# A shared score tile with nine products instead of twelve, row sums turned in spare columns, and products with V dealt 9 9 9 9 6 6 6 9 9

## The chip, the core and the metric

The kernel runs on one core of a Trainium2 chip. TensorE (PE in the profile, PEld for its weight loads) multiplies, VectorE (DVE) and ScalarE (ACT) read its results from PSUM, GpSimd (POOL) works on SBUF alone, and SyncE (SP) issues the DMAs. The metric is the device time of one execution in microseconds (us), the median of several runs; smaller is better.

## The reference

Three blocks follow each other. The change lies in the first.

```python
# q, k, v: (2, 8, 1152, 64) float32
q_pool = q.reshape(B, H, S // 2, 2, D).mean(axis=3)          # 576 query rows per head
scores = scale * np.matmul(q_pool, k.transpose(0, 1, 3, 2))  # 576 x 1152 per head
attn = np.exp(scores - np.max(scores, axis=-1, keepdims=True))
attn = attn / (np.sum(attn, axis=-1, keepdims=True) + 1e-09)
attn_out = np.matmul(attn, v)                                # 16 heads
# then x (1152 x 512) -> ELU block (512 -> 2048 -> 512)
# then RMS norm -> gated SiLU block (512 -> 1536 -> 512)
```

## The kernel before

Nearly every product is made of three: each fp32 operand is split into a high part in the fast format fp32r and a low part (the rest, again in fp32r), and high x high, high x low and low x high are added up in PSUM. `hi_...` makes a high part, `lo_...` subtracts it to make the low one (lines 60 to 70; these lines stand for all such operations in the profile: L61 and L64 on POOL, L67 and L70 on DVE).

The attention half works on pairs of heads, p = 0 to 7, with j = 0 and 1 for the two heads of a pair. Keys lie in a tile `kd` of 128 partitions: the high part of the 64 rows in partitions 0 to 63, the low part in 64 to 127. Queries (the pooled sum of two rows, in 576 columns) lie in `qt`: 128 partitions that hold the same 64 rows twice, once as high part (u = 0) and once as low part (u = 1), so a score tile of 128 queries takes two products over 1152 keys, each cut into three matmuls of 384 columns: six matmuls. A head has 576 queries, four tiles of 128 and a rest of 64. The rests of both heads of a pair share one tile, number 2 (`M`): its queries are set off by zero columns, and it takes both heads' two products, twelve matmuls.

One step of the loop (line 580) handles one score tile, nine steps to a pair:

- PE: the scores of this step's tile into the PSUM tile `s` (`emit_S`, L350; three banks, one buffer);
- PE: nine transposes of the tile two steps back (`do_T`, `emit_T`, L368; three PSUM buffers `t`);
- PE: eight products with V (`do_AV`, L394), taken from a queue of groups. A group has 18: nine blocks of keys, each with the high and the low part of the weights. A pair has four groups, two of 256 and two of 320 columns; a group enters the queue when the last of its tiles has been transposed. Where the next group is not there yet, fewer are issued; where a transpose would overwrite what a waiting group still reads, the rest of that group is issued first;
- DVE: one reduction that takes the scores out of PSUM and finds the row's extreme (L354), three subtractions for the transposed tile (L70), an addition where a group of 256 columns ends (L414);
- ACT: three casts of the transposed tile (L376), copies where a group ends (L407 to L413), the exponential with the row sum (L359);
- POOL: a preparation of q, k or v for the pairs to come, by the table `plan` (L487); SP fetches the raw array of the preparation that follows (`fetch`; two buffers for raw k and v together, two for raw q).

When all nine tiles of a pair are transposed, `emit_r` takes the reciprocals of the row sums. They lie along partitions and are needed along columns: POOL spreads them (`rs`), four transposes turn eight of the nine columns two steps after the pair's last product with V, a further transpose the ninth column a step later (`emit_scale`, L433 and L438), ACT copies them out of PSUM into `xs`. In the steps in which that is due, the transposes of the score tile come after the products with V and not before them. `emit_x` then scales the pair's output on POOL and splits it. In pair 0 the tiles come in the order 0 1 3 4 2 5 6 7 8, in the others as 0 to 8. In some steps (`early_ops`) weights of the next half are converted ahead.

Of the kernel before, what the change touches and what calls it, by code (L numbers as in the profile page):

```python
# [39 lines left out]
def tile_kernel(ctx: ExitStack, tc: tile.TileContext, qd, kd, vd, w1d, w2d, wgd, wvd, wod, rgd, outd):  # L40
# [229 lines left out]
    qt = [ap.tile([128, 2, 704], F32R, name=f"qt{i}", tag=f"qt{i}") for i in range(3)]  # L270
# [5 lines left out]
    for z in qt:  # L276
        V.memset(f(z[:, :, 0:64]), 0.0)
        V.memset(f(z[:, :, 640:704]), 0.0)
    V.memset(ones, 1.0)

# [19 lines left out]
    def prep_q(p, j, t, eng, cols=((0, QS),)):  # L300
# [4 lines left out]
        d, qp = QD[p, j], t[:, 0, :]  # L305
# [18 lines left out]
    def prep_v(p, j, t, eng):  # L324
        hi, lo = eng
        d = VD[p, j] = ap.tile([128, 9, 128], F32R, tag="vd", name="vd", bufs=3)
# [4 lines left out]

    st = {}
# [3 lines left out]
    def emit_S(p, i):  # L336
# [3 lines left out]
        if i == M:  # L340
            parts = [(QD[p, j][:, u, c:c + 128], KD[p, j]) for j, c in ((1, 0), (0, 576)) for u in (0, 1)]
        else:
            j, c, _, _, _ = TILES[i]
            parts = [(QD[p, j][:, u, c:c + 128], KD[p, j]) for u in (0, 1)]
# [17 lines left out]
    def emit_T(p, i):  # L362
        src = P.pop((p, i)).rearrange("p a b -> p (a b)")
        for g in range(3):
            ps = tbank()[:, 0:384].rearrange("p (k c) -> p k c", k=3)
# [10 lines left out]
            T.copy(oh, re(ps))  # L376
            lo_dve(ol, re(ps), oh)
# [40 lines left out]
    def emit_r(p):  # L418
        s = st[p]
        V.tensor_scalar(out=s[:, 2], in0=s[:, 1], scalar1=1e-9, scalar2=None, op0=ALU.add)  # L420
        V.reciprocal(s[:, 3], s[:, 2])
        rs[p] = ap.tile([128, 640], F32, tag="xs", name="rs", bufs=1)[:, 0:512].rearrange("p (a b) -> p a b", a=8)
        hi_pool(rs[p], s[:, 3, 0:8].to_broadcast([128, 8, 64]))
# [58 lines left out]
    def fetch(u):  # L482
        if u not in raws:
# [3 lines left out]
    plan = {1: lambda p: ("v", p, 0), 2: lambda p: ("q", p + 1, 1), 3: lambda p: ("k", p + 1, 1, 0),  # L487
            4: lambda p: ("k", p + 1, 1, 1), 5: lambda p: ("v", p + 1, 1), 6: lambda p: ("q", p + 1, 0),
            7: lambda p: ("k", p + 1, 0, 0), 8: lambda p: ("k", p + 1, 0, 1)}
    steps = [(p, i) for p in range(8) for i in ([0, 1, 3, 4, 2, 5, 6, 7, 8] if p == 0 else range(NPT))]  # L490
    ns = len(steps)
    jobs = {n: [] for n in range(-1, ns)}
    for n in range(ns):
# [4 lines left out]
        if k in plan and not (p == 0 and k == 1):  # L498
# [81 lines left out]
    for step in range(ns):  # L580
# [14 lines left out]
        if step >= LT and due:  # L595
            do_T(step)
# [507 lines left out]
```

## Time and profile before

| | us |
|---|---|
| median of 3 runs (lowest, highest) | 667.93 (667.74, 668.16) |
| span of the profiled execution | 666.8 |
| from the first score matmul of pair 2 to that of pair 7 | 148.73 |
| PE, DVE, ACT, POOL busy in the whole span | 659.0, 511.5, 465.2, 443.6 |

The span is that of one profiled execution, from its first instruction to its last; the timed runs are 1.1 us longer, with what lies around the span. A matmul's record shows when it started and a modelled end, and records overlap: what a matmul costs in a sequence is the distance between starts. In the timeline, neighbouring records of one kind are merged, with their number behind the x; "idle before" in brackets names what ended a wait.

### The profile page before, as it was taken

Reading aid. Unit: us, or ns where it says so; the run is one execution under the profiler, and the core shown is the slowest. Engines: PE = TensorE matmul, PEld = TensorE weight load, DVE = VectorE, ACT = ScalarE, POOL = GpSimd, SP = SyncE. Lnnn points to the kernel's source line nnn. Section 1 sums busy time; section 2 is a strip of 40 time slices with the busy share of each in tenths; the row PEclk is TensorE's granted clock in tenths of the full one; section 3 lists DMA queues with packets and bytes.
Section 4 is the critical chain, followed back from the end, with each engine's and each line's share of the span. In section 5 each row is a group of like instructions: output and inputs, shape, how many; then the busy total and the mean of one; then the engine's idle time right before and its main releaser. Section 6 shows DMA issues by size and latency. Waiting matters only on the chain.

```text
span 666.8 us, 11391 instructions
## 1 busy us (share of the span) xinstructions
PE 659.0 (99%) x4149; PEld 652.1 (98%) x4149; DVE 511.5 (77%) x884; ACT 465.2 (70%) x910; POOL 443.6 (67%) x407
## 2 busy tenths in 40 slices
PE   7999999999999999999999999999999999999997
PEld 6999999999999999999999999999999999999997
DVE  7989898998999878987786787688697786676200
ACT  6988888898988977848758668866766654564300
POOL 4999888989989323758776695665998874404200
PEclk9999999999999999999999999999999999999999
DMA  6432333233223101142141232110323322204100
GB/s 177 171 107 90 108 131 133 90 108 121 90 89 94 46 1 64 43 148 95 64 158 65 94 129 94 65 64 32 126 96 125 129 94 68 91 1 162 68 36 36
DMA packets 21624, 61.75 MB, mean 93 GB/s; under 512 B 2752, under 2 KB 5056, under 8 KB 21568
## 3 DMA queue, kind: packets, MB, share of 16 engines
q1 hardware_dynamic: 21568, 61.03, 27.9%
q8 instruction: 32, 0.52, 0.3%
q14 instruction: 24, 0.20, 0.1%
HBM read 58.66 MB, written 2.36 MB: 92 GB/s over the span
## 4 chain that ended last, share of the span: by engine, by line
PE 96%; POOL 1%; DVE 1%; DMA 1%; issue 0%; SPq 0%; ACT 0%; POOLq 0%; ACTq 0%
PE b L747 17%; PE b L217 14%; PE b L219 14%; PE b L218 14%; PE s L350 12%; PE o L394 11%; PE t L368 10%; DMA rawq<-in_q_dram 1%; PE t L433 1%; DVE p L354 0%; POOL kd L64 0%; POOL qt L64 0%; PE fb L217 0%; PE fb L219 0%; PE fb L218 0%
## 5 line engine op out<-in xcount | busy, mean ns | idle before, releaser
L64 POOL TENSOR_TENSOR wl<-wt,wh 128x512 fp32r<-128x512 f32 x68 | 91.1, 1340 | 83.9 <-ACT wh L184 79.0
L70 DVE TENSOR_TENSOR ptl<-t,pth 128x384 fp32r<-128x384 f32 x216 | 106.7, 549 | 4.9 <-ACT pth L376 4.5
L354 DVE TENSOR_SCALAR_CACHE_REDUCE p<-s 128x1152 f32<-128x1152 f32 x72 | 97.4, 1354 | 15.1 <-PE s L350 13.7
L376 ACT CAST pth<-t 128x384 fp32r<-128x384 f32 x216 | 89.2, 488 | 22.3 <-PE t L368 21.6
L350 PE MATMUL s<-kd,qt 128*128 128x384 f32 x480 | 98.7, 342 | 2.9 <-DVE p L354 1.4
L359 ACT ACTIVATE p<-p,st 128x1152 f32<-128x1152 f32 x72 | 91.5, 1271 | 0.5 <-DVE p L354 0.2
L217 PE MATMUL b<-xh,wh 128*128 128x384 f32 x260 | 87.7, 337 | 0.0
L350 PEld LDWEIGHTS s<-kd,qt 128*128 128x128 f32 x480 | 81.0, 188 | 6.6 <-DVE p L354 2.8
L219 PE MATMUL b<-xh,wl 128*128 128x384 f32 x260 | 87.5, 336 | 0.0
L218 PE MATMUL b<-xl,wh 128*128 128x384 f32 x260 | 87.4, 336 | 0.0
L394 PE MATMUL o<-pth,vd 128*128 128x256 f32 (+1 forms) x288 | 84.4, 315 | 0.0
L368 PE MATMUL t<-ident,p 128*128 128x128 f32 x648 | 82.5, 272 | 0.0
L394 PE MATMUL o<-ptl,vd 128*128 128x256 f32 (+1 forms) x288 | 78.6, 295 | 0.0
L368 PEld LDWEIGHTS t<-ident,p 128*128 128x128 f32 x648 | 75.0, 141 | 1.8
L120 ACT ACTIVATE we<-wr 128x512 uint32<-128x512 uint32 x68 | 45.4, 667 | 38.8 <-DMA wr<-in_w_dram 19.1
L131 DVE TENSOR_SCALAR wm<-wm 128x512 f32<-128x512 f32 x63 | 43.8, 695 | 20.3 <-ACT wm L122 20.3
L394 PEld LDWEIGHTS o<-pth,vd 128*128 128x128 f32 x288 | 54.3, 189 | 0.3
L122 ACT ACTIVATE wm<-wr 128x512 f32<-128x512 f32 x63 | 39.6, 628 | 21.4 <-DVE wt L136 21.3
L394 PEld LDWEIGHTS o<-ptl,vd 128*128 128x128 f32 x288 | 54.5, 189 | 0.0
L218 PEld LDWEIGHTS b<-xl,wh 128*128 128x128 f32 x260 | 48.8, 188 | 0.0
L217 PEld LDWEIGHTS b<-xh,wh 128*128 128x128 f32 x260 | 48.8, 188 | 0.0
L219 PEld LDWEIGHTS b<-xh,wl 128*128 128x128 f32 x260 | 48.8, 188 | 0.0
(198 smaller groups left out, 1750.6 us busy)
## 6 DMA issues: line engine op xcount, KB each, us to landing
wr<-in_w_dram SPq DMA_DIRECT2D x32, 512.0 KB, 3.2
rawq<-in_q_dram SPq DMA_DIRECT2D x15, 576.0 KB, 4.0
rawk<-in_k_dram SPq DMA_DIRECT2D x28, 288.0 KB, 2.9
wr<-in_wg_dram SPq DMA_DIRECT2D x12, 512.0 KB, 3.2
wr<-in_wv_dram SPq DMA_DIRECT2D x12, 512.0 KB, 3.2
wr<-in_wo_dram SPq DMA_DIRECT2D x12, 512.0 KB, 3.2
rawv<-in_v_dram SPq DMA_DIRECT2D x16, 288.0 KB, 2.9
out_dram<-o SPq DMA_DIRECT2D x12, 192.0 KB, 1.8
```

The source lines that it names most:

```text
L64: G.tensor_tensor(out=o, in0=i, in1=f(h), op=ALU.subtract)
L70: V.tensor_tensor(out=o, in0=i, in1=f(h), op=ALU.subtract)
L217: PE.matmul(out, lhsT=wh[:, k, :], rhs=ah, start=first and k == 0, stop=False)
L218: PE.matmul(out, lhsT=wh[:, k, :], rhs=al, start=False, stop=False)
L219: PE.matmul(out, lhsT=wl[:, k, :], rhs=ah, start=False, stop=last and k == 3)
L350: PE.matmul(s[:, m, 0:384], lhsT=a, rhs=b[:, 384 * m:384 * m + 384], start=n == 0, stop=n == len(parts) - 1)
L354: V.tensor_scalar(out=pt, in0=s[:, :, 0:384], scalar1=-0.0625, scalar2=None, op0=ALU.mult, op1=ALU.min, accum_out=st[p][:, 0, TILES[i][4], :])
L359: T.activation(out=pt, in_=pt, func=AF.Exp, scale=-1.0, bias=st[p][:, 0, TILES[i][4], :], accum_out=st[p][:, 1, TILES[i][4], :])
L368: PE.transpose(ps[:, k, :], src[:, 128 * b:128 * b + 128], ident)
L376: T.copy(oh, re(ps))
L394: PE.matmul(self.o[:, 0:self.N], lhsT=v[:, b, :], rhs=(pth, ptl)[u][:, g["buf"], b, g["c0"]:320], start=self.n == 0, stop=self.n == 17)
L747: PE.matmul(out, lhsT=a[x][:, k, :], rhs=b[y][:, k, :], start=first and (k, x, y) == (0, 0, 0), stop=last and (k, x, y) == (1, 1, 0), skip ...
```

## The change

The shared tile takes nine matmuls. Both rests' high parts are multiplied with the keys as before (two products, six matmuls). The two products with low parts become one: the low parts of both heads' rests stand in one 128 x 128 tile `bd`, head 1's in partitions 0 to 63 and columns 64 to 127, head 0's in partitions 64 to 127 and columns 0 to 63, zeros elsewhere, and a tile `zd` holds the high parts of both heads' keys, one above the other. `zd` is filled by two DMAs per pair from SBUF to SBUF (`stack_k`). The low part of the queries, now a tile of its own, no longer needs the rest's columns, which go into `bd` by a subtraction of their own.

The row sums are turned by one transpose of a 128 x 128 tile `rc` into unused columns (384 to 511) of the third PSUM buffer of a score tile's transposes; ACT copies nine rows back; five DMAs write them in the right order to DRAM, and two DMAs read them back, spread over 64 partitions each (`store_r`, `load_r`). The last pair keeps the old way. The scaling follows three steps after the last product with V, as before.

All pairs take the tiles in the order 0 1 3 4 2 5 6 7 8. The products with V are dealt out 9 9 9 9 6 6 6 9 9 over the nine steps. The score tile's transposes always come before the products with V. V of head 1 is prepared in the pair's second step, V of head 0 in its sixth (before: head 0 in the second, head 1 of the next pair in the sixth), with two buffers instead of three.

```diff
-    qt = [ap.tile([128, 2, 704], F32R, name=f"qt{i}", tag=f"qt{i}") for i in range(3)]
+    qt = [(ap.tile([128, 704], F32R, name=f"qh{i}", tag=f"qh{i}"), ap.tile([128, QS], F32R, name=f"ql{i}", tag=f"ql{i}"))
+          for i in range(3)]
+    bds = [ap.tile([128, 128], F32R, name=f"bd{i}", tag=f"bd{i}") for i in range(2)]
...
+    for z in bds:
+        G.memset(f(z), 0.0)
     V.memset(ones, 1.0)
+    rc = ap.tile([128, 128], F32, name="rc")
+    G.memset(rc, 1.0)
...
-            h, l = (d[:, u, 64 + a:64 + b] for u in range(2))
-            hi(h, qp[:, a:b])
-            lo(l, qp[:, a:b], h)
+            hi(h[:, 64 + a:64 + b], qp[:, a:b])
+            if a <= m < b:
+                lo(bds[p % 2][r, o:o + 64], qp[r, m:m + 64], h[r, 64 + m:128 + m])
+            for a, b in ((a, min(b, 512)),) if m else ((max(a, 64), b),):
+                if a < b:
+                    lo(l[:, a:b], qp[:, a:b], h[:, 64 + a:64 + b])
+
+    ZD = {}
+
+    def stack_k(p, j):
+
+        if p not in ZD:
+            ZD[p] = ap.tile([128, S], F32R, tag="zd", name="zd", bufs=1)
+        SP.dma_start(out=f(ZD[p][64 * (1 - j):64 * (2 - j)]), in_=f(KD[p, j][0:64]))
...
-            parts = [(QD[p, j][:, u, c:c + 128], KD[p, j]) for j, c in ((1, 0), (0, 576)) for u in (0, 1)]
+            parts = [(QD[p, j][0][:, c:c + 128], KD[p, j]) for j, c in ((1, 0), (0, 576))] + [(bds[p % 2], ZD[p])]
...
+            if turn and g == 2:
+                PE.transpose(bank[:, 384:512], rc, ident)
...
             T.copy(oh, re(ps))
+            if turn and g == 2:
+                T.copy(rc[0:NPT], bank[0:NPT, 384:512])
             lo_dve(ol, re(ps), oh)
...
+        V.reciprocal(rc[:, 0:NPT], s[:, 2].rearrange("p a b -> p (a b)"))
+        later.extend([(step + 1, rows), (step + 2, lambda: store_r(p)), (step + 3, lambda: load_r(p))])
...
+    def store_r(p):
+
+        d = RD[p] = dp.tile([2, QS], F32, tag="rd", name="rd", bufs=2)
+        for j in range(2):
+            for k in range(2):
+                n = j + 4 * k
+                SP.dma_start(out=d[j:j + 1, 320 * k:320 * k + 256].rearrange("p (k c) -> (p k) c", k=2), in_=rc[n:n + 3:2, :])
+        SP.dma_start(out=d[:, 256:320], in_=rc[8:9, :].rearrange("p (j c) -> p j c", j=2))
+
+    def load_r(p):
+        d = RD.pop(p)
+        xs = XS[p] = ap.tile([128, 640], F32, tag="xs", name="xs", bufs=1)
+        for j in range(2):
+            SP.dma_start(out=xs[64 * j:64 * j + 64, 0:QS], in_=d[j:j + 1, :].to_broadcast([64, QS]))
...
-    steps = [(p, i) for p in range(8) for i in ([0, 1, 3, 4, 2, 5, 6, 7, 8] if p == 0 else range(NPT))]
+    steps = [(p, i) for p in range(8) for i in (0, 1, 3, 4, 2, 5, 6, 7, 8)]
...
-        if step >= LT and not due:
+        due, done = [w for w in later if w[0] <= step and w[1] is not rows], []
+        if step >= LT:
             do_T(step)
...
-        do_AV(8, lambda p: later.extend([(step + 2, lambda: emit_scale(p, (0,))),
-                                        (step + 3, lambda: emit_x(p, emit_scale(p, (1,))))]), done)
-        if step >= LT and due:
-            do_T(step)
+        do_AV((9, 9, 9, 9, 6, 6, 6, 9, 9)[step % NPT], lambda p: later.append((step + 3, lambda: emit_x(p, XS[p]))), done)
...
+        for u in jobs.get(step - 2, []):
+            if u[0] == "k" and u[3] == 1:
+                stack_k(u[1], u[2])
```

In the program, PE's queue of pair 1 around the shared tile before (s is the PSUM tile of scores, qt_91 and qt_93 the queries of both heads, t the transposes, o the products with V):

```order
L350 MATMUL s<-kd,qt_93 128x384 x6
L350 MATMUL s<-kd,qt_91 128x384 x6
L394 MATMUL o<-pth,vd 128x320
L394 MATMUL o<-ptl,vd 128x320
L368 MATMUL t<-ident,p 128x128 x9
L394 MATMUL o<-pth,vd 128x256
L394 MATMUL o<-ptl,vd 128x256
```

The same place after:

```order
L369 MATMUL s<-kd,qh_95 128x384 x3
L369 MATMUL s<-kd,qh_91 128x384 x3
L369 MATMUL s<-zd,bd_98 128x384 x3
L390 MATMUL t<-ident,p 128x128 x9
L420 MATMUL o<-pth,vd 128x256
L420 MATMUL o<-ptl,vd 128x256
L420 MATMUL o<-pth,vd 128x256
L420 MATMUL o<-ptl,vd 128x256
L420 MATMUL o<-pth,vd 128x256
L420 MATMUL o<-ptl,vd 128x256
```

Twelve score matmuls became nine, the last three on `zd`, and a whole step's six products follow the transposes.

PE's queue where pair 0's row sums are turned, before (in pair 1's seventh and eighth steps):

```order
L350 MATMUL s<-kd,qt_91 128x384 x6
L433 MATMUL t<-ident,rs 128x128 x4
L394 MATMUL o<-pth,vd 128x256
L394 MATMUL o<-ptl,vd 128x256
L394 MATMUL o<-pth,vd 128x256
L394 MATMUL o<-ptl,vd 128x256
L368 MATMUL t<-ident,p 128x128 x9
L350 MATMUL s<-kd,qt_91 128x384 x6
L438 MATMUL t<-ident,st 128x128
L394 MATMUL o<-pth,vd 128x320
```

And after (in pair 1's third step):

```order
L369 MATMUL s<-kd,qh_95 128x384 x3
L369 MATMUL s<-kd,ql_96 128x384 x3
L390 MATMUL t<-ident,p 128x128 x9
L392 MATMUL t<-ident,rc 128x128
L420 MATMUL o<-pth,vd 128x256
```

The five transposes became one behind a score tile's nine, and these stand ahead of the products in every step.

SP's queue at the start, before (the rows from the load of the norm's weights on):

```order
L532 DMA rg<-in_rg_dram 128x4
L286 DMA rawq<-in_q_dram 128x1152
L294 DMA rawk<-in_k_dram 128x576 x2
L93 DMA wr<-in_w_dram 128x1024 x2
L297 DMA rawv<-in_v_dram 128x576
```

And after, up to the first turn of row sums:

```order
L579 DMA rg<-in_rg_dram 128x4
L328 DMA zd<-kd 64x1152 x2
L292 DMA rawq<-in_q_dram 128x1152
L300 DMA rawk<-in_k_dram 128x576 x2
L93 DMA wr<-in_w_dram 128x1024 x2
L292 DMA rawq<-in_q_dram 128x1152
L300 DMA rawk<-in_k_dram 128x576
L328 DMA zd<-kd 64x1152
L300 DMA rawk<-in_k_dram 128x576
L303 DMA rawv<-in_v_dram 128x576
L292 DMA rawq<-in_q_dram 128x1152
L328 DMA zd<-kd 64x1152
```

The copies into `zd` stand between the loads, the first two ahead of pair 1's queries.

## Rows read from the trace of the kernel before

**Rows 1.** The page's part 4: shares of the chain that ended last, by engine

```profile
PE 96%; POOL 1%; DVE 1%; DMA 1%; issue 0%; SPq 0%; ACT 0%; POOLq 0%; ACTq 0%
```

**Rows 2.** Busy times by stretches, pairs 2 to 6: sum, then mean of five

```profile
sum 148.73, PE 148.73 PEld 146.09 DVE 136.59 ACT 130.96 POOL 131.15; mean PE 29.75 PEld 29.22 DVE 27.32 ACT 26.19 POOL 26.23
```

**Rows 3.** PE's timeline in pair 4 (start, us, what): shared tile, next step

```profile
128.89 2.27 PE L350 MATMUL s<-kd,qt 128*128 128x384 f32 x12
131.00 0.31 PE L394 MATMUL o<-pth,vd 128*128 128x320 f32 x1
...
133.21 1.21 PE L350 MATMUL s<-kd,qt 128*128 128x384 f32 x6
134.26 1.14 PE L368 MATMUL t<-ident,p 128*128 128x128 f32 x9
135.16 0.36 PE L394 MATMUL o<-pth,vd 128*128 128x256 f32 x1
135.36 0.28 PE L394 MATMUL o<-ptl,vd 128*128 128x256 f32 x1
...
136.06 0.28 PE L394 MATMUL o<-ptl,vd 128*128 128x256 f32 x1
```

**Rows 4.** PE's timeline in pair 4: the turn of pair 3's row sums

```profile
143.18 0.60 PE L433 MATMUL t<-ident,rs 128*128 128x128 f32 x4
...
143.74 0.28 PE L394 MATMUL o<-ptl,vd 128*128 128x256 f32 x1
...
146.13 0.27 PE L438 MATMUL t<-ident,st 128*128 128x128 f32 x1
...
146.38 0.31 PE L394 MATMUL o<-ptl,vd 128*128 128x320 f32 x1
...
147.41 1.15 PE L368 MATMUL t<-ident,p 128*128 128x128 f32 x9
148.52 1.31 PE L350 MATMUL s<-kd,qt 128*128 128x384 f32 x6
```

**Rows 5.** Timeline of PE and DVE in pair 0: the step with two products

```profile
23.02 1.21 PE L350 MATMUL s<-kd,qt 128*128 128x384 f32 x6
...
24.27 1.36 DVE L354 TENSOR_SCALAR_CACHE_REDUCE p<-s 128x1152 f32<-128x1152 f32 x1 [0.21 <-PE s L350]
...
25.55 0.55 DVE L70 TENSOR_TENSOR ptl<-t,pth 128x384 fp32r<-128x384 f32 x1
...
25.69 0.62 PE L350 MATMUL s<-kd,qt 128*128 128x384 f32 x2 [0.24 <-DVE p L354]
```

**Rows 6.** DVE's timeline in pair 3: three subtractions and the addition behind them

```profile
109.17 1.49 DVE L70 TENSOR_TENSOR ptl<-t,pth 128x384 fp32r<-128x384 f32 x3
110.57 0.41 DVE L414 TENSOR_TENSOR xf<-o,olo 64x256 f32<-64x256 f32 x1
```

**Rows 7.** PE's timeline in pair 1: the shared tile

```profile
38.97 1.41 PE L350 MATMUL s<-kd,qt 128*128 128x384 f32 x7
40.81 1.15 PE L350 MATMUL s<-kd,qt 128*128 128x384 f32 x5 [0.43 <-POOL kd L64]
41.80 0.31 PE L394 MATMUL o<-pth,vd 128*128 128x320 f32 x1
```

**Rows 8.** Timeline of POOL and PE in pair 0: last K half, shared tile

```profile
13.23 0.67 POOL L61 TENSOR_SCALAR kd<-rawk 64x576 fp32r<-64x576 f32 x1
...
15.97 1.63 PE L350 MATMUL s<-kd,qt 128*128 128x384 f32 x8 [0.57 <-DVE p L354]
```

**Rows 9.** DMA issues by line: count, size, median us from issue to landing

```profile
rawk<-in_k_dram SPq DMA_DIRECT2D x28, 288.0 KB, 2.9
...
out_dram<-o SPq DMA_DIRECT2D x12, 192.0 KB, 1.8
rawk<-in_k_dram SPq DMA_DIRECT2D x4, 144.0 KB, 4.5
```

**Rows 10.** POOL's timeline in pair 5: the fill of the spread reciprocals

```profile
160.44 0.62 POOL L61 TENSOR_SCALAR rs<-st 128x512 f32<-128x512 f32 x1 [0.47 <-DVE st L421]
```

More of the change, by code (lines that the diff above doesn't have):

```diff
@@ L275, in tile_kernel @@
     make_identity(nc, ident)
-    for z in qt:
-        V.memset(f(z[:, :, 0:64]), 0.0)
-        V.memset(f(z[:, :, 640:704]), 0.0)
+    for z, _ in qt:
+        V.memset(f(z[:, 0:64]), 0.0)
+        V.memset(f(z[:, 640:704]), 0.0)
+    for z in bds:
+        G.memset(f(z), 0.0)
     V.memset(ones, 1.0)
+    rc = ap.tile([128, 128], F32, name="rc")
+    G.memset(rc, 1.0)
     KD, VD, QD = {}, {}, {}
@@ L325, in prep_v @@
         hi, lo = eng
-        d = VD[p, j] = ap.tile([128, 9, 128], F32R, tag="vd", name="vd", bufs=3)
+        d = VD[p, j] = ap.tile([128, 9, 128], F32R, tag="vd", name="vd", bufs=2)
         hi(d[:, :, 0:64], t)
@@ L330, in tile_kernel @@
     POOL, DVE = (hi_pool, lo_pool), (hi_dve, lo_dve)
+    dp = actx.enter_context(tc.tile_pool(name="rdram", bufs=1, space=bass.MemoryType.DRAM))
     st = {}
@@ L340, in emit_S @@
         if i == M:
-            parts = [(QD[p, j][:, u, c:c + 128], KD[p, j]) for j, c in ((1, 0), (0, 576)) for u in (0, 1)]
+            parts = [(QD[p, j][0][:, c:c + 128], KD[p, j]) for j, c in ((1, 0), (0, 576))] + [(bds[p % 2], ZD[p])]
         else:
             j, c, _, _, _ = TILES[i]
-            parts = [(QD[p, j][:, u, c:c + 128], KD[p, j]) for u in (0, 1)]
+            parts = [(QD[p, j][u][:, c - 64 * u:c - 64 * u + 128], KD[p, j]) for u in (0, 1)]
         first = (p, i) == (0, 0)
@@ L360, in emit_exp, with emit_T @@
                      accum_out=st[p][:, 1, TILES[i][4], :])
-    def emit_T(p, i):
+    rows = []
+    def emit_T(p, i, turn=False):
         src = P.pop((p, i)).rearrange("p a b -> p (a b)")
         for g in range(3):
-            ps = tbank()[:, 0:384].rearrange("p (k c) -> p k c", k=3)
+            bank = tbank()
+            ps = bank[:, 0:384].rearrange("p (k c) -> p k c", k=3)
             for k in range(3):
@@ L497, in tile_kernel @@
             jobs[n] = u + jobs[n]
-        if k in plan and not (p == 0 and k == 1):
+        if k in plan and not (p == 0 and k in (1, 5)):
             u = plan[k](p)
@@ L554, in do_T @@
         pt, it = steps[step - LT]
+        turn = [w for w in later if w[0] <= step and w[1] is rows]
+        for w in turn:
+            later.remove(w)
         if avq and any(overwrites(it, a.g) for a in avq):
@@ L557, in do_T @@
             avq[0].emit(18)
-        emit_T(pt, it)
+        emit_T(pt, it, bool(turn))
     def do_AV(k, then, done=None):
@@ L580, in tile_kernel @@
     for step in range(ns):
+        if step == 3:
+            stack_k(0, 1)
+            stack_k(0, 0)
         emit_S(*steps[step])
@@ L585, in tile_kernel @@
             tbank = lambda: tp.tile([128, 512], F32, tag="t", name="t", bufs=3)
-        due, done = [w for w in later if w[0] <= step], []
-        if step >= LT and not due:
+        due, done = [w for w in later if w[0] <= step and w[1] is not rows], []
+        if step >= LT:
             do_T(step)
```

16 lines of the change are left out of this document (10 added, 6 removed).

## The prediction

> **What bounds the kernel now.** I read the chain of work that ended last first: TensorE (PE) holds 96% of the span, nearly all of it matmuls and transposes of both halves of the program [rows 1]. So time is won only where PE gets less to do or waits less, and lost only where PE waits more. The change touches the attention half alone, so I cut that half into pairs of heads. From pair 2 to pair 6 the table by stretches gives 148.73 us for five pairs, 29.75 us each; VectorE (DVE) is busy for 27.32 of these, ScalarE (ACT) for 26.19, GpSimd (POOL) for 26.23 [rows 2]. Nobody is far from PE: a pair cannot become much shorter than some 27 us whatever PE saves. A busy PE says little here, since its records overlap; I therefore read PE's timeline by starts. What the reader is to see there is what one step costs in sequence: six score matmuls, nine transposes, a share of the products with V.
>
> From starts: six score matmuls after other matmuls take 134.26 - 133.21 = 1.05 us, twelve of the fifth tile (tile 2 in the code) 131.00 - 128.89 = 2.11. Nine transposes take 0.90, and the matmul after them starts 0.20 instead of 0.117 after the first of its block, so a block of transposes costs 0.98 with the change of kind. A product with V is 0.117 with 256 columns (six spacings from 135.36 to 136.06) [rows 3] and 0.147 with 320 (seven from 146.38 to 147.41) [rows 4].
>
> **The change part by part**, against the profiled execution (span 666.8; the median of the runs, 667.93, is 1.1 more, which I keep as what lies around the span).
>
> *Nine score products.* Of the twelve matmuls of the shared tile three go: a half of 1.05, so 0.53. Eight tiles: **4.24 us**, all on PE's path.
>
> *The turn of the row sums.* Now four transposes and later one more per pair. The four with the change of kind: 143.74 - 143.18, less one product at 0.117, is 0.44. The single one: 146.38 - 146.13, less one at 0.147, is 0.10 [rows 4]. In their place one transpose at the end of a block that is there anyway, 0.11. Net 0.44 for each of seven pairs (the last keeps the old way): **3.08**. In the trace each of the four also has a duration, 0.60 us for the four of them [rows 4], but they overlap, so spacing counts. The Trainium skill, "TensorE: Matmul & The Clock Gate", Part 4: PE-mode transpose, prices a transpose in a kernel at about 275 ns; by that the 28 saved would give 7.7 instead of 3.1 and the time would be 654.7. The trace does not agree: the four, change of kind and all, take 0.44.
>
> *The stall beside it.* In the second step of the turn the transposes stand behind the products, and the next scores come 148.52 - 147.41 = 1.11 after them instead of 0.90 [rows 4]: PE waits for DVE to empty the one PSUM tile of scores. With transposes always ahead of the products 0.21 goes, seven times: **1.47**.
>
> *The fifth tile later in the pair.* From pair 1 on it moves from third to fifth place. In pair 1 its twelve matmuls took 41.80 - 38.97 = 2.83, with a wait for POOL's second K half in the middle [rows 7]; two steps later that half is long there: **0.72**.
>
> *The dealing.* 9 9 9 9 6 6 6 9 9 makes each of the four groups of 18 end with a step. The count per pair, 72, stays. In pair 0 the old dealing left a step with two products, in which PE waited for DVE: 25.69 - 23.02 = 2.67 where the work is 1.05 + 0.98 + 0.23 [rows 5]. That is 0.4, and 0.1 in the step behind it (an estimate): **0.5**.
>
> Gains: 4.24 + 3.08 + 1.47 + 0.72 + 0.5 = 10.0 us.
>
> Steps of a pair afterwards, by the same prices: first, second, eighth, ninth 1.05 + 0.98 + 9 x 0.147 = 3.35; third and fourth 3.08; fifth 1.58 + 0.98 + 0.70 = 3.26; sixth and seventh 2.73; with the turn 28.4 in all. The mean pair of before, 29.75, is within 0.2 of 28.4 + 0.53 + 0.44 + 0.21.
>
> *What can eat it: the short steps.* The tile of scores has one buffer. Its loop, with nothing else late, is that 2.67: scores from 23.02, DVE's reduction from 24.27 for 1.36, next scores at 25.69 [rows 5]. Against 2.73 (and 3.20 against 3.26 in the fifth step, whose reduction starts 0.53 later) only 0.06 us are to spare in three steps of each pair. DVE's own work there is 25.55 - 24.27 = 1.28 for the reduction and 110.57 - 109.17 = 1.40 for three subtractions [rows 6], 2.68 together: it fits, barely. DVE's 64x256 addition lands behind the fourth and seventh steps, where the next reduction has 0.3 and more. I charge 0.04 for each of 24 steps, **1.0**; bounds 0 and 0.21 (the stall of today) each, 5.0 in all.
>
> *K by DMA.* Two copies of half a K (64x1152, SBUF to SBUF) per pair, issued by SP behind loads that already wait for the same POOL work. No row shows such a copy; loads of the same 288 KB land in 2.9 us, those of the start in 4.5 [rows 9]. In steady state it has about 9 us of room (POOL ends K in the first or second step, PE wants it in the fifth). In pair 0 it has none: POOL's copy of K ends at 13.23 + 0.67 = 13.90, the copy lands between 16.8 and 18.4, and PE wants it six matmuls after 15.97, at 17.0 [rows 8, 9]. Cost 0 to 1.4; I take **0.4**, nearer to 2.9, since SP has little else in flight then. Behind the two copies in SP's queue stands the load of the next queries, whose POOL work comes several us later.
>
> *Row sums by way of DRAM.* Five small stores, two broadcast loads on SP. Nobody on PE's path waits: the result is first used by POOL, three steps later. POOL loses the 0.62 us fill [rows 10] and gains two 64x64 subtractions, which I bound by that 0.62; ACT loses three copies and gains one; the three zero and one fills lie in POOL's wait for its first load. Nothing, with POOL's and ACT's spare time as cover; what it costs without cover is the second rival.
>
> Sum: 10.0 - 1.0 - 0.4 = 8.6. 667.9 - 8.6 = **659.3 us** (span 658.2).
>
> **Rivals.** *First: the single tile of scores sets the short steps.* If DVE comes 0.2 late in them (a wait for ACT's cast, a conversion of weights), the stall of 0.21 appears in all 24: 5.0 instead of 1.0, **663.3**. For it: 0.06 to spare, DVE at 27.3 of a pair that shrinks to 28.4. Against it: the longer steps around lend it 0.3 to 0.7. It decides as soon as a reduction starts 0.06 late. The Trainium skill, "Perfetto Trace Analysis", section Matmuls, asks that independent matmul groups rotate through PSUM banks so that emptying one overlaps the next; these scores do not, and [rows 5] shows the wait that follows. Chance 0.20.
>
> *Second, on the other side: SP starves POOL.* The loads of the row sums wait in SP's queue until the stores have landed, and the next raw K and V are queued behind. Stores 1.8, loads 2.9 [rows 9]: up to 4.7 us per pair without a fetch. POOL needs 26.23 - 0.62 = 25.6 of work per pair, so 4.1 of idle time is where its round passes 29.75 and the kernel becomes slower. With 4.7 on top of some 1.7 that it waits for loads or for PE anyway, its round is 32.0: 2.3 over for seven pairs, 16, less about 9 that K and V are prepared ahead, some 7: **675**. Against it: the raw loads wait for a buffer from POOL for most of that time anyway. Chance 0.05.
>
> *Third: the change does not do what it says*, because the copied K is late in every pair and the fifth tile waits for it as pair 1's does now, 0.72 x 8 = 5.8: **665.1**. It would take a copy of over 9 us. Chance 0.05.
>
> **How the numbers follow.** Forecast 0.66, first rival 0.20, third 0.05, second 0.05; 0.04 for no change, by several small things. The range reaches from 657.0 (no cost, and the 0.2 per pair of small waits that a clean pair does not have) to 664.3, the first rival with a start that costs its full 1.4. A measurement of this kernel tells 0.2% (1.3 us) from no change; so faster 0.91, same 0.04, slower 0.05.
>
> **What would show it.** Right: the profile of the changed kernel has nine score matmuls of the fifth tile in about 1.6 us; pairs 2 to 6 at 28.4 to 28.6; PE's waits named by DVE's reduction, if any, in the fifth to eighth steps; one wait of under a microsecond for the copied K at 17 us; and the second half of the program as long as before. Wrong: pairs of 29 us with a wait of 0.1 to 0.3 in each short step (first rival); POOL idle for DMAs and PE waiting for POOL's K or V (second); PE waiting for the copied K in every pair (third); or a second half that gives time back.

## The result

The changed kernel takes **661.52 us** (median of 4 runs, 661.02 to 662.38) against 667.84 for the kernel before beside it (667.30 to 668.16): a ratio of 0.9907, 95% interval 0.9895 to 0.9918. Forecast were 659.3, range 657.0 to 664.3. The profiled execution has a span of 659.4.

TensorE holds the chain as before; the page's part 4, as [rows 1]:

```profile
PE 95%; DVE 2%; DMA 1%; ACT 1%; issue 1%; SPq 0%; DVEq 0%; ACTq 0%
```

PE's waits in the whole program, but for one of the warm-up at the start (what, for what: us in total, times, longest):

```profile
PE s L369 <- DVE p L373: 2.8, 5, 0.9
```

No wait for POOL's K or V and none for the copied K stands among them. The table by stretches, one pair each from first score matmul to first score matmul, answers [rows 2] (columns: length, busy time of each engine with its instructions, granted clock, DMA share, GB/s):

```profile
60.50:89.17 28.67, 28.67 (x213) 28.38 (x212) 27.28 (x52) 24.92 (x52) 25.44 (x26) 1.00 0.48 135
...
118.04:147.75 29.71, 28.86 (x213) 28.36 (x212) 28.40 (x52) 25.04 (x52) 27.16 (x29) 1.00 0.43 131
...
sum 144.74, PE 143.83 PEld 141.62 DVE 136.23 ACT 127.56 POOL 129.97; mean PE 28.77 PEld 28.32 DVE 27.25 ACT 25.51 POOL 25.99
```

Five pairs take 144.74 instead of 148.73. One of them, pair 4, is a microsecond longer than its neighbours: it gained nothing over before. Pair by pair, from start of pair to start of pair (the last one to the first matmul of the next half), with the forecast's terms in the last column (0.53 + 0.44 + 0.21, less the charge of 1.0 / 8, for a pair from 2 to 7):

| | before | after | change | forecast |
|---|---|---|---|---|
| start to pair 1 | 32.25 | 31.86 | -0.39 | -0.5 |
| pair 1 | 30.40 | 28.64 | -1.76 | -1.8 |
| pair 2 | 29.66 | 28.67 | -0.99 | -1.05 |
| pair 3 | 29.80 | 28.87 | -0.93 | -1.05 |
| pair 4 | 29.72 | 29.71 | -0.01 | -1.05 |
| pair 5 | 29.85 | 28.90 | -0.95 | -1.05 |
| pair 6 | 29.70 | 28.59 | -1.11 | -1.05 |
| pair 7 | 33.80 | 32.57 | -1.23 | -1.05 |
| sum | 245.18 | 237.81 | -7.37 | -8.6 |

The rest of the program is as long as it was: 421.6 us from that matmul to the end in both. So between these two profiled executions 7.4 us were gained where 8.6 were forecast, and nearly all of the difference is pair 4; between the medians it is 6.3.

The fifth step of pair 2 in PE's timeline (start, us, what), which answers [rows 3]:

```profile
73.55 1.21 PE L369 MATMUL s<-kd,qh 128*128 128x384 f32 x6
74.59 0.68 PE L369 MATMUL s<-zd,bd 128*128 128x384 f32 x3
75.11 1.15 PE L390 MATMUL t<-ident,p 128*128 128x128 f32 x9
...
76.79 0.39 PE L369 MATMUL s<-kd,qh 128*128 128x384 f32 x1
```

Nine score matmuls take 75.11 - 73.55 = 1.56, the step 3.24 (forecast 1.58 and 3.26). The turn, in the third step, answers [rows 4]:

```profile
68.31 1.15 PE L390 MATMUL t<-ident,p 128*128 128x128 f32 x9
69.29 0.27 PE L392 MATMUL t<-ident,rc 128*128 128x128 f32 x1
69.32 0.36 PE L420 MATMUL o<-pth,vd 128*128 128x256 f32 x1
```

Ten transposes take 1.01 instead of 0.90: the 0.11 of the forecast.

### The profile page after: what moved, and what is told of

The parts are those of the page before. It is cut to its first block, busy times and chain, and to the rows that moved or that the text cites. A ratio compares the mean times of both kernels' runs of the same rounds, so it can differ in the third digit from the quotient of the medians.

```text
span 659.4 us, 11417 instructions
## 1 busy us (share of the span) xinstructions
PE 651.7 (99%) x4097; PEld 645.8 (98%) x4097; DVE 510.2 (77%) x884; ACT 460.0 (70%) x896; POOL 442.4 (67%) x417
## 4 chain that ended last, share of the span: by engine, by line
PE 95%; DVE 2%; DMA 1%; ACT 1%; issue 1%; SPq 0%; DVEq 0%; ACTq 0%
PE b L800 18%; PE b L217 15%; PE b L219 15%; PE b L218 15%; PE s L369 11%; PE o L420 11%; PE t L390 10%; DMA rg<-in_rg_dram 1%; DMA rawk<-in_k_dram 1%; DVE ptl L70 0%; PE fb L217 0%; PE fb L219 0%; PE fb L218 0%; DVE p L373 0%; PE b L768 0%
## 5 line engine op out<-in xcount | busy, mean ns | idle before, releaser
L420 PE MATMUL o<-pth,vd 128*128 128x256 f32 (+1 forms) x288 | 82.2, 308 | 0.0
L420 PE MATMUL o<-ptl,vd 128*128 128x256 f32 (+1 forms) x288 | 80.0, 300 | 0.0
L369 PE MATMUL s<-kd,qh 128*128 128x384 f32 x240 | 56.1, 346 | 2.9 <-DVE p L373 2.8
L217 PE MATMUL b<-gh,wh 128*128 128x384 f32 x144 | 48.4, 336 | 0.0
```

The source lines that it names most:

```text
L217: PE.matmul(out, lhsT=wh[:, k, :], rhs=ah, start=first and k == 0, stop=False)
L369: PE.matmul(s[:, m, 0:384], lhsT=a, rhs=b[:, 384 * m:384 * m + 384], start=n == 0, stop=n == len(parts) - 1)
L420: PE.matmul(self.o[:, 0:self.N], lhsT=v[:, b, :], rhs=(pth, ptl)[u][:, g["buf"], b, g["c0"]:320], start=self.n == 0, stop=self.n == 17)
```

## What holds pair 4 up

PE, DVE and POOL in the third step of pair 4, by their timelines of the changed kernel:

```profile
124.74 1.43 POOL L64 TENSOR_TENSOR kd<-rawk,kd 64x576 fp32r<-64x576 f32 x1
125.34 0.86 DVE L446 TENSOR_SCALAR st<-st 128x9 f32<-128x9 f32 x1
126.23 0.22 DVE L452 RECIPROCAL rc<-st 128x9 f32<-128x9 f32 x1
126.24 0.86 POOL L436 TENSOR_TENSOR xf<-xf,olo 64x320 f32<-64x320 f32 x1
126.36 1.29 DVE L133 SCALAR_TENSOR_TENSOR wt<-wt,we 128x512 uint32<-128x512 uint32 x1
127.08 1.11 POOL L61 TENSOR_SCALAR vd<-rawv 128x576 fp32r<-128x576 f32 x1
127.58 1.34 DVE L373 TENSOR_SCALAR_CACHE_REDUCE p<-s 128x1152 f32<-128x1152 f32 x1
...
128.99 0.79 PE L369 MATMUL s<-kd,qh 128*128 128x384 f32 x3 [0.85 <-DVE p L373]
```

and the same place in pair 2:

```profile
65.89 1.43 POOL L64 TENSOR_TENSOR kd<-rawk,kd 64x576 fp32r<-64x576 f32 x1
...
67.82 0.16 DVE L446 TENSOR_SCALAR st<-st 128x9 f32<-128x9 f32 x1
...
68.15 0.63 DVE L133 SCALAR_TENSOR_TENSOR wt<-wt,we 128x512 uint32<-128x512 uint32 x1
```

The addition to nine row sums takes 0.16 in pair 2 and 0.86 in pair 4, where POOL's K subtraction runs until 124.74 + 1.43 = 126.17; the addition ends at 126.20. The conversion of weights takes 0.63 and 1.29: POOL's next operation ends at 127.10, the conversion 0.55 later. It goes both ways: POOL's cast of V, 0.67 elsewhere, takes 1.11 there. DVE's reduction, which reads PSUM, keeps its 1.34 beside POOL. Behind the two small operations stands the reduction, and PE waits for that one.

Not every DVE operation within SBUF is held. The reciprocal of the same nine row sums takes 0.21 to 0.22 in every trace, also where POOL is at work, as in pair 4 of the changed kernel's second trace (e1 below), by the timelines of POOL and DVE:

```profile
124.99 1.43 POOL L64 TENSOR_TENSOR kd<-rawk,kd 64x576 fp32r<-64x576 f32 x1
125.08 0.21 DVE L452 RECIPROCAL rc<-st 128x9 f32<-128x9 f32 x1
125.22 1.75 DVE L133 SCALAR_TENSOR_TENSOR wt<-wt,we 128x512 uint32<-128x512 uint32 x1
```

The reciprocal runs beside POOL's subtraction; the conversion behind it ends at 126.97, again 0.55 after POOL's end at 126.42.

The Trainium skill, "SBUF — State Buffer", section "SBUF: two separate sides", says that VectorE and GpSimd have one pair of ports in common, and that a GpSimd operation, or one of VectorE in a two-port mode or with two inputs in SBUF, holds it whole while the other blocks; the trace agrees for the addition and the conversion, with the end of the addition 0.03 behind POOL's.

## The experiments

Three runs of the changed kernel itself lie between 661.5 and 662.8 (medians; single runs 661.0 to 663.2), so each kernel is set beside the one of its own chip: 662.79 for e2 to e4, 661.73 for e6 to e8. Beside e9 to e12 the changed kernel was not run. Where the times cannot tell two kernels apart, the steps in the trace can, though each kernel has one trace; a clean pair of the changed kernel, one in which no step waits, is 28.6 to 28.7.

> The changed kernel as it is, beside which the next three stand. Both theories: 661.5 us again (661.0 to 662.4). It also tells by how much the timed run is longer than its span, which was 1.9 us in the result where I had reckoned with 1.1: if the scratch tile in DRAM or the extra DMAs cause it, the kernel before has 1.1 in this call and this one 1.9; if it is the profile's own offset, both have the same.

Measured: 662.79 (662.01 to 663.02), ratio 0.9922 (0.9908 to 0.9937), above the range expected. Its time is 1.8 to 1.9 above its span, and so is that of the kernel before (1.74 to 1.86), so the new DMAs add nothing around the span. Third steps of pairs 4 and 6 at 3.98 and 4.30, in place of 3.21.

**The three parts, one undone at a time.** The old turn of the row sums:

```diff
-        V.reciprocal(rc[:, 0:NPT], s[:, 2].rearrange("p a b -> p (a b)"))
-        later.extend([(step + 1, rows), (step + 2, lambda: store_r(p)), (step + 3, lambda: load_r(p))])
+        V.reciprocal(s[:, 3], s[:, 2])
...
+        hi_pool(rs[p], s[:, 3, 0:8].to_broadcast([128, 8, 64]))
```

> The old turn of the row sums (POOL's fill, four transposes and one, ACT's copies, transposes of the score tile behind the products where it is due), nine score products and the new dealing kept, no scratch tile in DRAM. Theory 1 (what PE no longer does is paid in full, by the spacings of its starts): + 0.44 + 0.21 for each of seven pairs, 4.5 in all, 666.1. Theory 2 (in the three short steps DVE's round of about 2.8 us sets the time): the transposes of the old turn now fall into two short steps, where PE waits some 0.13 per pair anyway, so + 0.3 and a stall of 0 to 0.2: 2.2 to 3.6 in all, 663.7 to 665.1. If the scratch tile costs time outside the span, the timed run comes to 1.1 over its span again.

Measured: 666.68 (663.36 to 668.43, 10 runs). A clean pair has 29.16 to 29.23, 0.55 more than 28.63: seven times that is 3.9, and the medians differ by 3.9 too, which proves little: the runs scatter by 5 us. Forecast were 3.08 + 1.47 = 4.55. POOL has its fill of 0.61 [rows 10] back in the third step, and in pair 4 that step took 5.21, with the conversion of weights at 2.50. Four of the ten runs, all four above 667, have a mean granted clock of 0.996 to 0.997, the others 0.999 to 1.0; which of the two, clock or time, follows the other is not shown.

Twelve score products, without the copies of K:

```diff
-            parts = [(QD[p, j][0][:, c:c + 128], KD[p, j]) for j, c in ((1, 0), (0, 576))] + [(bds[p % 2], ZD[p])]
+            parts = [(QD[p, j][u][:, c:c + 128], KD[p, j]) for j, c in ((1, 0), (0, 576)) for u in (0, 1)]
```

> Twelve score products in the shared tile again (low parts of the queries with zero borders, no stacked K, no copies of K), the new turn and dealing kept. Theory 1: + 0.53 for each of eight tiles, 4.2, so 665.7. Theory 2: pair 0's tile stands behind DVE's work in both kernels, so seven tiles, 3.7, and the fifth step with its longer scores takes some of the DVE lateness off the sixth, up to 0.1 per pair: 2.9 to 3.7, 664.4 to 665.2.

Measured: 664.09 (663.91 to 664.21), 1.3 above the changed kernel. Both theories were too high. The fifth step has its price, 3.78 against 3.24 in every pair from 1 to 7, but no other step of pairs 1 to 6 is longer than in a clean pair, and pairs 1 to 6 are 29.11 to 29.17. Of the 3.8 that the seven fifth steps save, e1 loses 3.1 in pairs 2 to 6 (28.60, 29.21, 29.50, 29.10, 29.82). In e3's trace, on the other hand, the half that follows is 1.1 longer than in e1's (422.8 against 421.6), so the 1.3 between the medians is no price of three matmuls. In pair 0 nothing is saved: 3.89 with twelve, 3.97 with nine. The timeline of PE and DVE of the changed kernel shows why, and answers [rows 8]:

```profile
15.51 1.28 PE L369 MATMUL s<-kd,qh 128*128 128x384 f32 x6 [0.57 <-DVE p L373]
16.65 0.77 PE L369 MATMUL s<-zd,bd 128*128 128x384 f32 x3
16.84 1.22 DVE L70 TENSOR_TENSOR vd<-rawv,vd 128x576 fp32r<-128x576 f32 x1
17.26 1.14 PE L390 MATMUL t<-ident,p 128*128 128x128 f32 x9
...
19.48 0.77 PE L369 MATMUL s<-kd,qh 128*128 128x384 f32 x3 [0.34 <-DVE p L373]
```

The copied K comes at most 0.1 late (16.65 - 15.51 = 1.14 for six matmuls), but DVE's preparation of V stands before the reduction, and PE waits for that at the end of the step.

Eight products with V in every step:

```diff
-        do_AV((9, 9, 9, 9, 6, 6, 6, 9, 9)[step % NPT], lambda p: later.append((step + 3, lambda: emit_x(p, XS[p]))), done)
+        do_AV(8, lambda p: later.append((step + 3, lambda: emit_x(p, XS[p]))), done)
```

> The old dealing of eight products per step in all pairs, everything else as changed. Theory 1, as I had put it in the prediction: dealing counts only in pair 0, + 0.5, 662.0. Theory 2: with groups that end in the middle of a step the seventh step of every pair is left with two products, 1.05 + 0.98 + 0.23 = 2.27 of PE's work against a round of 2.67 to 2.8, so 0.4 to 0.5 in each of eight pairs, + 3.2 to 4.2, less what the sixth step gains by two products more (0.07 each): 664.2 to 665.2.

Measured: 665.83 (664.50 to 666.85): the dealing is worth 3.0 where 0.5 was forecast. (In the trace 1.0 of it lies in the half that follows, and pair 2 has a third step of 4.38; the clean pairs alone give 0.34 times seven, 2.4.) PE and DVE in pair 2's seventh step of this kernel:

```profile
82.45 1.15 PE L390 MATMUL t<-ident,p 128*128 128x128 f32 x9
82.65 1.36 DVE L373 TENSOR_SCALAR_CACHE_REDUCE p<-s 128x1152 f32<-128x1152 f32 x1 [0.21 <-PE s L369]
...
83.55 0.28 PE L420 MATMUL o<-ptl,vd 128*128 128x256 f32 x1
...
84.07 0.79 PE L369 MATMUL s<-kd,qh 128*128 128x384 f32 x3 [0.24 <-DVE p L373]
```

Two products with V, then PE waits for the tile of scores: 84.07 - 81.40 = 2.67, what [rows 5] shows for pair 0, here in every pair. A pair of 28.97 instead of 28.63.

Undone one at a time, the three parts cost 3.9, 1.3 and 3.0, 8.2 together, where the whole change brought 5.1 beside them (667.85 less 662.79): what they are worth does not add up.

The turn alone is both of the last two edits, so the new turn, the tile's fifth place and the new places of V's preparation remain (no run puts V back):

> Of the three parts of the change only the turn of the row sums (with the fifth place of the shared tile): twelve score products, eight products with V in every step. Theory A (the parts add up as in the prediction: turn 3.1, stall beside it 1.5, the fifth place 0.7): 662.7 to 663.5, a pair 29.1. Theory B (without the old turn the old dealing leaves a seventh step with two products with V that waits for the tile of scores, 0.4 per pair, as the eight-per-step kernel shows it): a pair 29.4 to 29.5, the time 665.5 to 666.7.

Measured: 669.39 (668.88 to 670.42, 10 runs), ratio 1.0024 (1.0015 to 1.0033): slower than before, and slower than either theory. A clean pair has 29.50, as theory B says; the seventh step 2.67 with two products. In the kernel before the four old transposes stood in the seventh step, beside four products, and filled it (2.86); taking them out saves 0.19 there and not 0.44. Pairs 4 and 6 have third steps of 4.15 and 4.12 in place of 3.38, with the conversion of weights at 1.77 and 1.74; pair 2's is 3.70, and the first steps of pairs 5 and 7 have 4.00 and 3.89 in place of 3.52. And 1.2 us are lost in the half that follows, at two waits of PE for DVE some 74 us behind its start, which the kernel before does not have; e3 loses 1.0 there too, and e6 0.7. What shifts that place was not tried.

**The short steps.** One of three subtractions left out where `cut` is set, in the fifth to seventh steps:

```diff
-            lo_dve(ol, re(ps), oh)
+            if not (cut and g == 1):
+                lo_dve(ol, re(ps), oh)
```

> The changed kernel without one of VectorE's three low-part subtractions in the fifth, sixth and seventh steps of pairs 1 to 7 (so a third of those steps' low parts is left out of the result). It shortens VectorE's round there by 0.47, from 2.79 to 2.32. Theory A (VectorE's round of a reduction of 1.28 and three subtractions of 1.51 sets the sixth and seventh steps): they fall from 2.79 to 2.73, which is TensorE's own work, or to 2.67 to 2.73 where the turn-round of the one tile of scores is next; the sixth steps of pairs 3, 5 and 7 fall from 3.0 to 2.8; the time by 0.8 to 1.6, to 660 to 661. Theory B (the turn-round of the tile of scores sets them): sixth and seventh steps stay at 2.79, the time at 661.5 to 662.

Measured: 661.96 (661.66 to 663.01). Its third steps of pairs 2, 4 and 6 take 4.29, 4.21 and 3.92, so the time says little; the short steps do. In the changed kernel DVE has no gap in these steps, by its timeline in pair 2:

```profile
76.59 1.48 DVE L70 TENSOR_TENSOR ptl<-t,pth 128x384 fp32r<-128x384 f32 x3
78.10 1.36 DVE L373 TENSOR_SCALAR_CACHE_REDUCE p<-s 128x1152 f32<-128x1152 f32 x1
...
79.38 1.48 DVE L70 TENSOR_TENSOR ptl<-t,pth 128x384 fp32r<-128x384 f32 x3
80.89 1.36 DVE L373 TENSOR_SCALAR_CACHE_REDUCE p<-s 128x1152 f32<-128x1152 f32 x1
```

a round of 80.89 - 78.10 = 2.79, which looks like the bound, since the steps last 2.79. It is not. Without the subtraction DVE idles, by its timeline of e9 (in brackets the idle time before the row):

```profile
79.16 1.36 DVE L373 TENSOR_SCALAR_CACHE_REDUCE p<-s 128x1152 f32<-128x1152 f32 x1 [0.49 <-PE s L369]
```

and the sixth and seventh steps of clean pairs are still 2.75 to 2.81. Theory B is nearer. PE has no gap there either: its six score matmuls take 77.90 - 76.79 = 1.11, where they take 82.45 - 81.40 = 1.05 in e4. That is the 0.06 between 2.79 and 2.73. Why they take longer is not settled; their weights are loaded later behind the matmul before them than elsewhere (79.517 against its start at 79.479, elsewhere 0.003 behind it), 0.14 after DVE has gone on to its next operation. What the experiment does remove is the stall in the sixth steps of pairs 3, 5 and 7, from 3.06, 3.00 and 2.94 to 2.82, 2.84 and 2.77. That stall comes from ACT's cast of weights, which stands before the casts for which DVE waits (the changed kernel, pair 3):

```profile
104.49 0.61 ACT L184 CAST wh<-wt 128x512 fp32r<-128x512 f32 x1
105.12 1.25 ACT L400 CAST pth<-t 128x384 fp32r<-128x384 f32 x3
...
105.63 1.49 DVE L70 TENSOR_TENSOR ptl<-t,pth 128x384 fp32r<-128x384 f32 x3 [0.32 <-ACT pth L400]
```

**Why POOL is late in pair 4.** POOL's waits in the changed kernel between 60 and 215 us:

```profile
POOL xf L436 <- ACT xf L435: 4.4, 5, 1.3
POOL vd L61 <- DMA rawv<-in_v_dram: 2.6, 3, 1.0
POOL rawq L314 <- DMA rawq<-in_q_dram: 2.0, 2, 1.4
```

The queries of 576 KB come 1.4 late in pair 3. SP issues the weights' 512 KB (93.60) just ahead of them (94.04), the copied K (94.77) and the next raw K (96.29) behind. In e3, which has no copies, that wait is not there. In the three traces of the changed kernel the third step of the pair that follows is long where the queries of pair 3 or 5 come 1.4 or more late, and only there (1.4 and 0.6 here, 2.1 and 1.5 in e1, 1.9 and 0.8 in e5).

> The changed kernel once more, as the measure for the three kernels beside it: 661.0 to 663.0, with the third step of pair 4 or 6 at 4.0 to 4.3 us in place of 3.2 where GpSimd's K subtraction still runs when VectorE comes to the conversion of weights.

Measured: 661.73 (661.48 to 663.15). Pair 4's third step 4.65, more than expected, the queries 1.9 late.

The load of weights moved behind the copies:

```diff
+        ws.hold = NPT <= step < 8 * NPT - 1
         ws.step(0, early_ops.get(steps[step], 0))
+        if step % NPT == 2:
+            ws.load(ws.want)
```

> One thing is moved: the 512 KB load of weights in pairs 3, 5 and 7 is issued behind the copies of K and the next raw K, where it stood ahead of the raw queries. Theory A (the queries' 576 KB share the DMA engines with the weights and the copied K, come 1.4 to 2.1 us late in pairs 3 and 5, make GpSimd late, and its K subtraction then holds up VectorE's small operations one pair later): GpSimd's wait for the raw queries goes, the third steps of pairs 4 and 6 fall from 4.0 to 4.3 to 3.2, the time falls by 1.0 to 2.3 to about 660. Theory B (GpSimd is late by its own 1.28 us of weight work in pairs 3 and 5, whatever the loads do): the third steps stay at 4.0 to 4.3 and the time at 661.0 to 663.0.

Measured: 661.32 (660.14 to 661.92). The wait for the queries is gone, and pair 4 reads, in the timelines of DVE and POOL:

```profile
124.21 1.44 POOL L64 TENSOR_TENSOR kd<-rawk,kd 64x576 fp32r<-64x576 f32 x1
...
126.04 0.17 DVE L450 TENSOR_SCALAR st<-st 128x9 f32<-128x9 f32 x1
...
126.37 0.63 DVE L134 SCALAR_TENSOR_TENSOR wt<-wt,we 128x512 uint32<-128x512 uint32 x1
```

The third steps of pairs 2, 4 and 6 are 3.21, as theory A says, with POOL's weight work of 1.28 where it was. But pair 3 loses 0.35 at its first two steps (3.63 and 3.46): there another of DVE's operations on weights (L137, 0.68 alone) takes 1.73 and ends 0.55 behind POOL's subtraction of the queries. The move spares one place, not every one. Pairs 1 to 6 together take 172.6 against 174.0 in e5. The median gives only 0.4 of that, within the scatter of either kernel: this profiled execution started 0.8 later into pair 1 than e5's, and its second half is 0.5 longer.

The suspected cause put in on purpose:

```diff
+            if step % NPT == 8 and u[0] == "k" and u[1] > 1:
+                for _ in range(3):
+                    lo_pool(xb[64:128], f(xb)[64:128], xb[64:128])
```

> The suspected cause is put in on purpose: behind the last K subtraction of pairs 2 to 7 GpSimd does three subtractions of 64x192 more, in a tile of their own that nobody reads, some 0.5 us each. Theory A (a VectorE operation that needs the port that GpSimd holds stands until GpSimd's operation ends): VectorE's 0.16 us addition in the third step takes 0.5 to 1.2, the 0.63 us conversion 1.1 to 1.8, the third steps of pairs 2, 4 and 6 rise from 3.2 to 3.7 to 4.6, those of pairs 3, 5 and 7 by at most 0.4; the time rises by 2 to 4, to 664 to 666. Theory B (the two are late together only because both wait for the same transfer): VectorE's operations keep 0.16 and 0.63, the third steps their 3.2, the time 661.5 to 662.5.

Measured: 663.21 (662.08 to 664.49), below what theory A says and above theory B. The operations follow theory A: the addition takes 0.65 to 1.20 in all of pairs 1 to 5, where the changed kernel has it long in pair 4 alone, and the third steps of pairs 2, 4 and 6 are 3.78, 3.95 and 4.02; the conversion, at 0.82, 0.83 and 1.78, is mostly held less than expected. The time is no measure of it. The 1.3 to e9, which ran beside it, do not come from the third steps, since e9 has longer ones without the added work, but from fifth steps (below). Pair 4 in the timelines of DVE and POOL (the second row is the addition, the third the added work):

```profile
126.59 1.43 POOL L64 TENSOR_TENSOR kd<-rawk,kd 64x576 fp32r<-64x576 f32 x1
127.01 1.05 DVE L448 TENSOR_SCALAR st<-st 128x9 f32<-128x9 f32 x1
127.98 2.01 POOL L64 TENSOR_TENSOR xb<-xb 64x192 fp32r<-64x192 f32 x3
...
128.22 0.83 DVE L133 SCALAR_TENSOR_TENSOR wt<-wt,we 128x512 uint32<-128x512 uint32 x1
```

It also shows the third rival, which the change itself does not: in pairs 3 and 5 K is then late enough for the copy to be waited for, and the fifth step has 4.47 and 4.07 for 3.24 (PE's timeline of e10, pair 3):

```profile
105.07 0.79 PE L371 MATMUL s<-zd,bd 128*128 128x384 f32 x3 [0.95 <-DMA zd<-kd]
```

Over the traces of e1, e5, e6, e9, e12 and the changed kernel, the third steps of pairs 2, 4 and 6 follow from one number, the end of POOL's K subtraction, counted from the step's start. Up to 0.87 (eight steps) the step has 3.21. At 1.10, 1.12, 1.38, 1.41, 1.47 (twice), 1.49, 1.82 and 1.83 it has 3.92, 3.94, 4.21, 4.23, 4.29 (twice), 4.30, 4.64 and 4.65: the end and 2.82. One case lies off it (2.11 and 3.98, pair 4 of e1 as shown above): there the addition slipped in between two of POOL's operations, and only the conversion was held.

**Candidates.** DVE's conversion a step earlier and ACT's cast behind the short steps (e7, the lines for pairs 2 and 3), with the later load as well (e8), and the casts and the load without the conversion (e12):

```diff
-    early_ops = {(0, 7): 1, (1, 1): 1, (1, 8): 1, (2, 1): 1, (2, 8): 2, (3, 1): 1, (3, 2): 1, (3, 3): 2, (3, 4): 1,
+    early_ops = {(0, 7): 1, (1, 1): 1, (1, 8): 1, (2, 0): 1, (2, 8): 2, (3, 1): 1, (3, 3): 2, (3, 7): 2,
```

> One thing is moved: VectorE's conversion of weights in pairs 2, 4 and 6 stands one step earlier, and ScalarE's cast of weights in pairs 3, 5 and 7 behind the short steps. Theory A (the conversion is held up by GpSimd's K subtraction, which is late in pairs 4 and 6 only at the third step): the third steps of pairs 4 and 6 at 3.2 to 3.9 (VectorE's other small operation may still be held for up to 0.7), the sixth steps of pairs 3 and 5 back from 3.0 to 2.8, the time lower by 1.0 to 2.0, at 660 to 661. Theory B (the conversion is held up wherever it stands, since GpSimd has hardly a gap): the stall of about 1 us moves to the second step, the sixth steps alone give 0.5, the time is 661 to 662.5.

Measured: 661.98 (660.78 to 663.69). The third steps of pairs 4 and 6 are 3.29 and the sixth ones 2.79 to 2.80, as theory A says, but the conversion is held a step earlier too, as theory B says (1.78 and 1.54 for 0.63, with second steps of 3.97 and 3.72 for 3.37). Besides, the queries come up to 2.7 late, K with them, and the fifth steps of pairs 3 and 5 wait for DMAs, 3.71 and 4.51 (the trace names the copied K for one wait, the small stores beside it for the other).

> Both moves of the two kernels before it at once. Theory A (late queries make GpSimd late, and GpSimd's subtraction holds up VectorE): no step of pairs 1 to 7 over its clean length but by 0.1, a pair 28.6, the time 659.3 to 660.3. Theory B (GpSimd is late by its own work and VectorE is held up wherever the conversion stands): 661 to 662.5.

Measured: 662.01 (660.51 to 662.47). The profiled execution has the shortest pairs of all (28.63, 28.63, 28.63, 28.82, 28.86, 28.60) and a span of 658.4, near theory A; the other three runs have spans of 659.6 to 660.3, which puts the median into theory B's range, and their traces are not there to tell why.

> A candidate: the load of weights behind the copies of K, and ScalarE's cast of weights in pairs 3, 5 and 7 moved behind the short steps, while VectorE's conversion stays where the change has it. Theory A (queries that land late and casts that stand before the exponentials of the short steps are what pairs of over 28.63 us wait for): pairs 28.6 to 28.8, the time 659.8 to 660.8. Theory B (what is gained there is given back, since another VectorE operation meets GpSimd, or the weights come late): 661 to 662.

Measured: 662.57 (662.06 to 663.84). Sixth steps 2.77 to 2.79, but the third steps of pairs 2, 4 and 6 are 3.94, 4.29 and 4.64: with the cast, POOL's 1.28 of weight work moved directly ahead of K in pairs 3 and 5, and in pair 1 the queries were 1.6 late. Theory B. None of the candidates beats the changed kernel by what the runs can tell. The three with the cast moved (e7, e8, e12) also have times 2.07 to 2.18 above their spans, where all others have 1.74 to 1.90: 0.3 that no step shows, and that stay unexplained.

## Why the prediction was near, and where it was off

The sign was right, and the size within a third (6.3 us gained, 8.6 forecast); the pieces were not all what they were said to be, and some errors cancelled. Of its own signs of being right, nine matmuls in about 1.6 and an unchanged second half came; pairs 2 to 6 at 28.4 to 28.6 did not (28.59 to 28.90, and 29.71), and PE's longest wait fell into a third step, not into the fifth to eighth. By its own steps:

**What lies around the span** was taken as 1.1, the median of the runs less the span of one profiled execution. In 38 executions of before beside the experiments the time is 1.74 to 1.86 above the span, and the median span is 666.1. So the execution of [rows 1] was some 0.7 longer than usual: the prices were read from it, but their sum was taken from a median of usual ones. Of the 2.2 us between 659.3 and 661.5 that is 0.7. Where in that execution the 0.7 lie is not shown, since the kernel before has one trace.

**Nine products** were forecast at 0.53 for each of eight tiles. Seven give 0.54 (3.78 to 3.24); pair 0 gives 0.1 (4.08 to 3.97 us), since DVE's subtraction of V bounds that step: 0.4 too much. The start hides it: up to its fifth step it became 0.46 shorter, since the load for which POOL waits landed that much earlier in this execution (POOL starts at 8.13 instead of 8.59), and behind that 0.07 longer. That it comes out near its forecast (-0.39 for -0.5) is luck; e1 and e5 reach pair 1 at 31.15 and 31.48. Undone alone, in e3, nine products are worth 1.3 and not 4.2, for the reasons told there.

**The turn, the stall beside it and the dealing** were forecast at 3.08, 1.47 and 0.5, and these pieces are wrong. By clean pairs the way goes from 29.66 (before) by the turn alone to 29.50, by the dealing to 29.13, by nine products to 28.63: 0.16, 0.37 and 0.50. The turn's 0.65 a pair was priced as if what leaves the seventh step were time won; but [rows 5] showed that a step with two products takes 2.67 and not 2.26, and the forecast used that row for pair 0 only. It did not ask what the seventh step of the other pairs becomes when the turn leaves it. With the new dealing, 0.53 of the 0.65 come out, and the sum was near because the dealing is part of the change: two wrong prices that offset each other.

**Pair 1's wait** was forecast at 0.72 and is gone: before, the shared tile's step took 5.03 there and 4.33 in pair 2.

**The short steps** were charged 0.125 a pair. A clean pair has 28.63, 0.23 over the 28.4 built from prices; half of it is the sixth and seventh steps (2.79 for 2.73, twice). So 0.1 a pair too little, which the 0.17 that before's mean pair had over its own prices gave back. The forecast feared DVE's round and the turn-round of the tile of scores; e9 shows that it is not DVE's round.

**The first rival** came in three places, not 24: the sixth steps of pairs 3, 5 and 7 wait 0.15 to 0.3 for DVE, which waits for ACT behind a cast of weights, the first of the two reasons that the text named.

**The second rival** came in a form that the forecast had not costed. It said that SP would keep raw data from POOL until POOL's round is longer than PE's. POOL was late by 1.4 once and caught up within a pair, which costs PE nothing by itself. But POOL that is late works at another time, and DVE's small operations then wait for it: 1.0 in pair 4 of the profiled execution, 1.9 in pairs 4 and 6 of e1, 1.4 in pair 4 of e5. This is the step of the forecast that is missing, not one that is mis-sized: it counted what each engine has to do and what it waits for, and nothing for two engines that are only at work at the same time. The trace of before had the sign of it, in rows that the forecast did not show: the same addition takes 0.16 in pairs 2, 3, 4 and 6, 0.72 in pair 5 and 1.09 in pair 1, and PE does not wait for it there.

**The third rival** did not come with the change (in e10 it does); **the copied K of pair 0** costs at most 0.1 of the 0.4.

So of the 2.2 us between 659.3 and 661.5, 0.7 lie around the span, 1.0 in pair 4, 0.2 in the other pairs and the start together, and 0.3 are the distance of the median from the profiled execution (659.4 + 1.8 = 661.2).

## What to carry to other kernels

Cost a change as new steps put together whole, not as a list of savings: what leaves a step may have been filling it, and part of this change alone was slower than no change. A long-run mean hides which operation has two durations: look for an operation whose minimum and maximum differ although its shape does not, and see what ran beside it. And where the answer is to be within a microsecond, take what lies around the span from runs that list both, not from one profile and a median.

## What the runs showed of the hardware

Two of DVE's operations with all their data in SBUF, a TENSOR_SCALAR on 128x9 and a SCALAR_TENSOR_TENSOR on 128x512, stood until POOL's running operation had ended (0.16 became up to 1.29, 0.63 up to 2.50), and POOL's cast stood for DVE's (0.67 became 1.11). A RECIPROCAL on 128x9 in SBUF did not stand (0.21 to 0.22 beside POOL); reductions and subtractions that read PSUM went on at 1.36 and 0.55. Where loads of 512, 576 and 288 KB and a copy of 288 KB were issued within 3 us, the second of them took 8.1 us (issued at 93.54, used at 101.67 in e1), although SP had issued the copy behind it; without the copy (e3) or with the 512 KB behind it (e6) nobody waited for it. Six score matmuls took 1.11 instead of 1.05 where DVE had left the tile they write only 0.14 before their first weights were loaded.
